# A kernel of gated linear attention and two expert layers: the prologue in another order, the first masks on ScalarE and GpSimd, products of ones ahead

## The chip, the cores and the metric

The kernel runs on one core of one Trainium2 chip. The metric is the device time of one execution in microseconds (us), the median of the runs shown. The engines are named as in the profile: PE is TensorE's matmuls, PEld its weight loads, DVE is VectorE, ACT ScalarE, POOL GpSimd, SP SyncE. SP issues nearly all transfers.

## What is computed

Three layers follow one another, on 3072 tokens (4 batches of 768) with 8 heads of 48:

```python
# 1. gated linear attention, per batch and head
f = sigmoid(f_logit)
for t in range(768):
    state = f[t][:, None] * state + outer(k[t], v[t])
    y[t] = q[t] @ state
# 2. dense layer, d_ff = 2048
h = maximum(x @ w_in, 0); x = (h * h) @ w_out
# 3. one of 8 experts per token (argmax of x @ w_gate), d_ff = 1024
out[mask] = gate[mask] * (maximum(x[mask] @ w1[e], 0) @ w2[e])
```

## The kernel before

**Tiling.** The tokens are cut into 24 chunks of 128 (`C`), and three chunks make a group of 384 (`G`); there are 8 groups. A chunk of attention is done in steps: `load_chunk` (f, q and k, v by SP), `sigmoid` (ScalarE, L210), `decays` (VectorE: two scans over 517 columns and a reciprocal, L216 to L225), `scale_qk` (VectorE, three products, keys first, L235 to L237), `scores` (TensorE: the keys' transposes into `pk`, L257, copied by ScalarE to `kt`, L259; then 16 products into two banks `pa`, L264), `masked` (VectorE multiplies both banks with a triangular mask into `at`, L271), `outputs` (TensorE: the queries with the state, L300, keys with values into `pu`, L310, values with masked scores into `py`, L320; then ScalarE's copies into `xT`, L328 to L333) and `state` (VectorE, L345 to L348). In group 0 the rows of heads 6 and 7 are brought to their places in `xT` by three products with the constant `spread` (L331); in later groups two small transfers xT<-xT do that (L336).

**The dense layer.** For each group `moe_h` makes 16 hidden blocks `ph` (L395 in group 0, where the weights are used whole; L405 in later groups, where weights and inputs are split into a high and a low part), `moe_act` squares their positive part on ScalarE (L411, L412), and `moe_out` adds them to `po` (L435), two blocks later. `ps_h` has two banks for hidden blocks, `ps_o` one for each of the three `po`, `ps_a` three that attention's steps share.

**Weights.** The dense weights come as 64 bit numbers in 16 jobs of 768 KB, alternately of `w_in` and `w_out`. `stage_job` loads one into one of three buffers `stg`, `convert_job` turns it into 32 bit with three VectorE instructions (L167, L170, L173) and has the next but two loaded into the buffer that it frees; `split_job` later splits it. Job 0 serves hidden blocks 0 and 1, job 1 their output blocks, job 2 hidden blocks 2 and 3, and so on.

**Order.** On TensorE, ScalarE, VectorE and GpSimd the order of this part is that of the program (`manual_schedule`, from L566 on); the constants ahead of it, and SP's queue in all of it, are ordered by the framework's planner. An engine works through its queue in order, so an instruction that waits holds all behind it. In the prologue chunks 0, 1 and 2 are done one after the other, with the first three conversions between the steps of chunk 2 and the decays, state and scaling that prepare chunk 3. Then group 0 of the dense layer runs, and the three chunks of the next group are threaded into its 16 blocks: `attention_group` waits for pairs (block, place in the block), and chunk 3 has its scores at block 1, chunks 4 and 5 at blocks 6 and 10; decays, outputs and scaling follow one, two and three blocks later. Each of blocks 0 to 12 of group 0 also converts one job (3 to 15). After job 15 the space of `stg` is freed and a table `wgb` of 1.5 MB is loaded (L787). At block 14 `split_x` splits the next group's `xT` into `xh` (ScalarE, L162) and `xl` (VectorE, L163).

## Time and profile before

| | us |
|---|---|
| median of three runs | 805.46 |
| the runs | 803.75, 805.46, 805.48 |
| the profiled execution | 804.5 |
| its span, first to last instruction | 802.8 |

The profile shows one execution. Its times are counted from the first instruction, so 1.7 us of the execution lie outside the span. A row of the timeline or of the chain begins with its start and its duration in us; what stands in brackets at its end is the idle time of the engine before it and what ended that.

### The profile page before, as it was taken

To read this page: it belongs to the slowest core of one execution; us is meant where nothing else is said; L and a number is where in the kernel's file an instruction comes from. 1 tells how busy PE (TensorE), PEld (TensorE's weight loads), DVE (VectorE), ACT (ScalarE), POOL (GpSimd) and SP (SyncE) were. 2 spreads that over 40 slices of the span, in tenths; PEclk is the share of its full clock that TensorE was granted. 3 is DMA by queue.
4 is the path that set the end of the run, shared out by engine and by line. 5 is a ranking of instruction groups with operands and counts; after the bars stand their busy time and mean duration, and the time that the engine had idled before them with its cause. 6 is when DMAs were issued, how large, how long until landed. Compare 5 with 4: busy or idle time off the path is not lost.

```text
span 802.8 us, 15135 instructions
## 1 busy us (share of the span) xinstructions
PE 775.1 (97%) x5657; PEld 723.2 (90%) x5657; DVE 561.3 (70%) x1309; ACT 413.4 (51%) x822; POOL 76.2 (9%) x108
## 2 busy tenths in 40 slices
PE   5899999999999999999999999999999999999994
PEld 4566579999999999999999999998999999999994
DVE  7999689768757767857757844668566676666650
ACT  2224376454464454455455454762566666666651
POOL 2000000000000000000000002000432232223110
PEclk9999999999999999999999999999999999999997
DMA  9787511111130121130120015321877777776760
GB/s 274 216 262 231 142 40 41 52 53 51 40 91 26 45 82 46 45 101 27 46 71 1 1 39 199 110 76 52 289 221 224 220 219 228 211 213 208 212 205 18
DMA packets 39410, 98.93 MB, mean 123 GB/s; under 512 B 5502, under 2 KB 9314, under 8 KB 39200
## 3 DMA queue, kind: packets, MB, share of 16 engines
q1 hardware_dynamic: 35744, 88.42, 37.3%
q0 software_dynamic: 3584, 9.46, 3.3%
q8 instruction: 46, 0.75, 0.4%
q14 instruction: 36, 0.29, 0.1%
HBM read 88.16 MB, written 10.24 MB: 123 GB/s over the span
## 4 chain that ended last, share of the span: by engine, by line
PE 85%; issue 6%; DVE 4%; DMA 2%; POOL 1%; ACT 1%; POOLq 0%; SPq 0%; DVEq 0%; ACTq 0%
PE po L435 25%; PE ph L405 23%; PE ph L982 11%; PE qo L1002 11%; PE ph L395 3%; PE pa L264 3%; PE py L320 3%; PE py L300 1%; PE pu L310 1%; DMA xT<-xT 1%; PE px L642 1%; PE pk L257 1%; DMA out<-o,ids 1%; PE pl L485 0%; DVE tl L216 0%
## 5 line engine op out<-in xcount | busy, mean ns | idle before, releaser
L411 ACT ACTIVATE gg<-ph 128x384 f32<-128x384 f32 x128 | 62.8, 491 | 184.6 <-PE ph L405 134.0
L614 DVE TENSOR_TENSOR w_lo<-raw,w_hi 128x768 fp32r<-128x768 f32 x112 | 107.0, 957 | 31.7 <-ACT w_hi L613 31.7
L418 DVE TENSOR_TENSOR gl<-gg,gh 128x384 fp32r<-128x384 f32 x112 | 62.1, 555 | 85.3 <-ACT gh L416 84.0
L405 PE MATMUL ph<-xh,w_lo 128*128 128x384 f32 x336 | 118.7, 353 | 0.9 <-ACT gg L411 0.9
L405 PE MATMUL ph<-xl,w_hi 128*128 128x384 f32 x336 | 114.4, 341 | 0.6 <-DVE xl L163 0.6
L405 PE MATMUL ph<-xh,w_hi 128*128 128x384 f32 x336 | 113.9, 339 | 0.0
L435 PE MATMUL po<-w_hi,gl 128*128 128x384 f32 x336 | 113.4, 338 | 0.0
L435 PE MATMUL po<-w_hi,gh 128*128 128x384 f32 x336 | 113.2, 337 | 0.0
L435 PE MATMUL po<-w_lo,gh 128*128 128x384 f32 x336 | 112.8, 336 | 0.0
L986 ACT ACTIVATE hh<-ph 128x256 fp32r<-128x256 f32 (+1 forms) x120 | 44.3, 370 | 103.3 <-PE ph L982 91.5
L613 ACT ACTIVATE w_hi<-raw 128x768 fp32r<-128x768 f32 x112 | 93.6, 837 | 0.0
L982 PE MATMUL ph<-xh,w_lo 128*128 128x256 f32 x312 | 88.9, 285 | 0.0
L982 PE MATMUL ph<-xl,w_hi 128*128 128x256 f32 x312 | 87.6, 281 | 0.0
L982 PE MATMUL ph<-xh,w_hi 128*128 128x256 f32 x312 | 87.5, 280 | 0.0
L459 DVE SCALAR_TENSOR_TENSOR junk<-rows,wgb 128x384 f32<-128x384 f32 x144 | 79.9, 555 | 3.3
L987 DVE SCALAR_TENSOR_TENSOR hl<-ph,hh 128x256 fp32r<-128x256 f32 (+1 forms) x120 | 48.7, 405 | 42.4 <-ACT hh L986 39.5
L1002 PE MATMUL qo<-w_hi,hl 128*128 128x384 f32 x208 | 70.4, 339 | 0.0
L1002 PE MATMUL qo<-w_hi,hh 128*128 128x384 f32 x208 | 70.4, 338 | 0.0
L1002 PE MATMUL qo<-w_lo,hh 128*128 128x384 f32 x208 | 70.1, 337 | 0.0
L412 ACT ACTIVATE gg<-gg 128x384 f32<-128x384 f32 x128 | 67.3, 526 | 4.1
L405 PEld LDWEIGHTS ph<-xh,w_lo 128*128 128x128 f32 x336 | 63.0, 188 | 6.9 <-issue 3.1
L405 PEld LDWEIGHTS ph<-xl,w_hi 128*128 128x128 f32 x336 | 63.1, 188 | 1.0 <-DVE xl L163 0.8
(235 smaller groups left out, 1498.0 us busy)
## 6 DMA issues: line engine op xcount, KB each, us to landing
raw<-w_e SPq DMA_DIRECT2D x120, 384.0 KB, 3.6
qk<-qk SPq DMA_DIRECT2D x46, 192.0 KB, 3.6
v<-vt SPq DMA_DIRECT2D x24, 256.0 KB, 3.7
stg<-w_in SPq DMA_DIRECT2D x8, 768.0 KB, 6.1
stg<-w_out SPq DMA_DIRECT2D x8, 768.0 KB, 6.0
f<-ft SPq DMA_DIRECT2D x24, 226.2 KB, 3.1
xs<-rows SPq DMA_DIRECT2D x8, 577.5 KB, 3.3
wgb<-w_gateT SPq DMA_DIRECT2D x1, 1536.0 KB, 7.1
```

Source lines behind the costliest of these rows:

```text
L405: nc.tensor.matmul(ph, lhsT=w[:, sl], rhs=x[:, k, :], start=(n == 0), stop=(n == 8))
L411: nc.scalar.activation(out=gg, in_=ph, func=AF.Relu)
L412: nc.scalar.activation(out=gg, in_=gg, func=AF.Square)
L418: nc.vector.tensor_tensor(out=gl, in0=gg, in1=gh.bitcast(F32), op=ALU.subtract)
L435: nc.tensor.matmul(po[m], lhsT=a[:, sl], rhs=w[:, ws], start=(i == 0 and n == 0), stop=(i == NF - 1 and n == len(terms) - 1),)
L459: nc.vector.scalar_tensor_tensor(out=junk, in0=rows[:, m, 0:DM], scalar=1.0, in1=wgb[0][:, e, :], op0=ALU.mult, op1=ALU.mult, accum_out=lg ...
L613: nc.scalar.activation(out=hi, in_=src, func=AF.Copy)
L614: eng.tensor_tensor(out=lo, in0=src, in1=hi.bitcast(F32), op=ALU.subtract)
L982: nc.tensor.matmul(ph, lhsT=wslice(s, w, (i * 3 + k) * 128, 128), rhs=x[:, k, :], start=(n == 0), stop=(n == 8))
L986: nc.scalar.activation(out=hh, in_=ph, func=AF.Relu)
L987: nc.vector.scalar_tensor_tensor(out=hl, in0=ph, scalar=0.0, in1=hh.bitcast(F32), op0=ALU.max, op1=ALU.subtract)
L1002: nc.tensor.matmul(out_t[s][m], lhsT=x[:, sl], rhs=wslice(s, w, 3 * F2 + i * DM, DM), start=(i == 0 and n == 0), stop=(i == 7 and n == 2),)
```

## The change

It does these things:

- Among the constants `step_r` and `step_f`, which the scans of `decays` read, come first on GpSimd, and `spread` after the masks.
- The input f of chunk 1 is loaded before v of chunk 0.
- `scores` is cut into `key_rows` (transposes and their copy) and `scores` (the 16 products), and `outputs` into `key_values`, `state_queries` and `scores_values`; the steps of the three first chunks then stand in a finer order, in which a chunk's products with `spread` come after the next chunk's scores.
- The outputs of the three first chunks go to the banks of `ps_o`, and their keys with values to the banks of `ps_h`, in place of `ps_a`. Row copies become three copies of 128 columns each.
- `masked` of chunks 0, 1, 3, 4 and 5 is done by two ScalarE copies and two GpSimd selects, in place of two VectorE products.
- 72 products of the constant `ones_bf` with itself stand first on TensorE, and 24 more before the values of chunk 0; nothing reads their results.
- The first three conversions stand together after chunk 2; decays 3 moves to block 0 of group 0, state 2 and the scaling of chunk 3 to block 1, and chunk 3's scores from block 1 to block 2.

The diff, without the loops that only moved into functions of their own:

```diff
--- before.py
+++ after.py
@@ -64,14 +64,13 @@
     xs = dram.tile([NT, ROW], F32, name="xs")
 
 
+    step_r = const.tile([PR, FL], BF16, name="step_r")
+    nc.gpsimd.memset(step_r, PFLOOR)
+    nc.gpsimd.memset(step_r[:, ::SEG], 1.0)
+    step_f = const.tile([PR, FL], F32, name="step_f")
+    nc.gpsimd.memset(step_f, PFLOOR)
     ident = const.tile([128, 128], F32, name="ident")
     make_identity(nc, ident)
-
-    spread = const.tile([128, 3, 128], F32, name="spread")
-    nc.gpsimd.memset(spread, 0.0)
-    for r in range(3):
-        for o in (0, 64):
-            nc.gpsimd.tensor_copy(spread[:, r, o + D : o + 64], ident[:, o + r : o + D : 3])
     mask = const.tile([128, 128], BF16, name="mask")
     nc.gpsimd.memset(mask, 1.0)
     nc.gpsimd.affine_select(
@@ -84,11 +83,12 @@
     )
     ones_bf = const.tile([128, 128], BF16, name="ones_bf")
     nc.vector.memset(ones_bf, 1.0)
-    step_r = const.tile([PR, FL], BF16, name="step_r")
-    nc.gpsimd.memset(step_r, PFLOOR)
-    nc.gpsimd.memset(step_r[:, ::SEG], 1.0)
-    step_f = const.tile([PR, FL], F32, name="step_f")
-    nc.gpsimd.memset(step_f, PFLOOR)
+
+    spread = const.tile([128, 3, 128], F32, name="spread")
+    nc.gpsimd.memset(spread, 0.0)
+    for r in range(3):
+        for o in (0, 64):
+            nc.gpsimd.tensor_copy(spread[:, r, o + D : o + 64], ident[:, o + r : o + D : 3])
     rev = const.tile([128, GC, NE], F32, name="rev")
     nc.gpsimd.iota(rev, pattern=[[0, GC], [-1, NE]], base=NE, channel_multiplier=0, allow_small_or_imprecise_dtypes=True)
     tok1 = const.tile([128, NCH], F32, name="tok1")
@@ -147,14 +147,22 @@
 
     ld_t = {}
 
+    def load_f(c):
+        f = ld.tile([PR, FL], F32, tag="f", name="f")
+        nc.sync.dma_start(out=f, in_=ft[c])
+        return f
+
+    f_t = {}
+
     def load_chunk(c):
         t = qk_t[c % 3]
-        f = ld.tile([PR, FL], F32, tag="f", name="f")
+        f = f_t.pop(c) if c in f_t else load_f(c)
         v3 = ld.tile([128, H, 64], F32, tag="v", name="v")
-        nc.sync.dma_start(out=f, in_=ft[c])
         for i in ((1, 2), (0, 1)) if c == 0 else ((0, 2),):
             for j in range(2):
                 nc.sync.dma_start(out=t[64 * j : 64 * j + D, slice(*i)], in_=qk[c, D * j : D * j + D, slice(*i)])
+        if c == 0:
+            f_t[1] = load_f(1)
         nc.sync.dma_start(out=v3, in_=vt[c])
         ld_t[c] = t, f, v3
 
@@ -247,9 +255,8 @@
 
     at_t = {}
 
-    def scores(c):
-        t, _, _ = ld_t[c]
-        qd, kd = t[:, 0], t[:, 1]
+    def key_rows(c):
+        kd = ld_t[c][0][:, 1]
         kt = None
         if c % CPB != CPB - 1:
             pk = ps_a.tile([128, 4, PR], F32, tag="att", name="pk")
@@ -257,84 +264,134 @@
                 nc.tensor.transpose(out=pk[:, p, :], in_=kd[:, p, :], identity=ident[0:PR, 0:PR])
             kt = a1.tile([128, 4, PR], F32, tag="kt", name="kt")
             nc.scalar.activation(out=kt, in_=pk, func=AF.Copy)
+        at_t[c] = kt, None
+
+    def scores(c):
+        t, _, _ = ld_t[c]
+        qd, kd = t[:, 0], t[:, 1]
         pas = [ps_a.tile([128, 4, 128], F32, tag="att", name="pa") for _ in range(2)]
         for p in range(4):
             for j in range(2):
                 rows = slice(64 * j, 64 * j + D)
                 nc.tensor.matmul(pas[j][:, p, :], lhsT=kd[rows, p, :], rhs=qd[rows, p, :], start=True, stop=True)
-        at_t[c] = kt, pas
+        at_t[c] = at_t[c][0], pas
+
 
     def masked(c):
         kt, pas = at_t[c]
         at = a1.tile([128, 2, 4, 128], F32, tag="at", name="at")
         for j in range(2):
-            nc.vector.tensor_tensor(
-                out=at[:, j], in0=pas[j], in1=mask[:, None, :].to_broadcast([128, 4, 128]), op=ALU.mult
-            )
+            if c in (0, 1, 3, 4, 5):
+                nc.scalar.activation(out=at[:, j], in_=pas[j], func=AF.Copy)
+                nc.gpsimd.affine_select(
+                    out=at[:, j],
+                    in_=at[:, j],
+                    pattern=[[0, 4], [1, 128]],
+                    compare_op=ALU.is_ge,
+                    fill=0.0,
+                    base=0,
+                    channel_multiplier=-1,
+                )
+            else:
+                nc.vector.tensor_tensor(
+                    out=at[:, j], in0=pas[j], in1=mask[:, None, :].to_broadcast([128, 4, 128]), op=ALU.mult
+                )
         at_t[c] = kt, at
 
 
...
+    def key_values(c, pu):
...
+    def state_queries(c, y, opens):
...
+    def scores_values(c, y, order, opens, closes):
+        _, _, v3 = ld_t.pop(c)
+        _, at = at_t.pop(c)
+        for n in order:
...
+    def outputs(c):
...
+        if not first:
+            state_queries(c, y, (0, 2))
+        if pu is not None:
+            key_values(c, pu)
+        scores_values(c, y, (2, 3, 0, 1), (0, 2) if first else (), (1, 3))
         ts = slice(m * C, (m + 1) * C)
         nc.scalar.activation(out=xT3[:, ts], in_=y[3], func=AF.Copy)
-        if g == 0:
-            for r in range(3):
-                nc.tensor.matmul(y[r], lhsT=spread[:, r, :], rhs=xT3[:, ts], start=False, stop=r > 0)
         nc.scalar.activation(out=xT[:, 2, ts], in_=y[2], func=AF.Copy)
         nc.scalar.activation(out=xT[:, 0:2, ts], in_=py[0], func=AF.Copy)
-        if m == GC - 1 and g:
+        if m == GC - 1:
             for o in (0, 64):
                 nc.sync.dma_start(out=xT[o + D : o + 64], in_=xT3[o : o + D])
+
+
+    first_y, first_pu = {}, {}
+
+    def first_banks(c):
+        po = [ps_o.tile([128, DM], F32, tag=f"po{m}", name="y") for m in range(GC)]
+        first_y[c] = [po[0][:, 0:C], po[0][:, C : 2 * C], po[2][:, 0:C], po[1][:, 0:C]]
+
+    def first_key_values(c):
+        first_pu[c] = pu = ps_h.tile([128, G], F32, tag="ph", name="pu")[:, 0 : 4 * D].rearrange(
+            "p (a b) -> p a b", a=4
+        )
+        key_values(c, pu)
+
+    def first_values(c, n=0):
+        y, ts = first_y[c], slice(c * C, (c + 1) * C)
+        for _ in range(n):
+            nc.tensor.matmul(y[3], lhsT=ones_bf, rhs=ones_bf, start=True, stop=True)
+        scores_values(c, y, (3, 2, 0, 1), () if c else (0, 2, 3), (3,))
+        nc.scalar.activation(out=x_t[0][1][:, ts], in_=y[3], func=AF.Copy)
+
+    def first_rows(c):
+        xT, xT3 = x_t[0]
+        y, ts = first_y[c], slice(c * C, (c + 1) * C)
+        for r in range(3):
+            nc.tensor.matmul(y[r], lhsT=spread[:, r, :], rhs=xT3[:, ts], start=False, stop=r > 0)
+        for r in (2, 0, 1):
+            nc.scalar.activation(out=xT[:, r, ts], in_=y[r], func=AF.Copy)
 
     def state(c, pu):
         if pu is None:
@@ -361,13 +418,22 @@
     def attention_group(g):
         for m in range(GC):
             c = g * GC + m
-            b = (1, 6, 10)[m] if g == 1 else 5 * m
+            b = (2, 6, 10)[m] if g == 1 else 5 * m
+            if c == GC:
+                while not (yield) == (0, 1):
+                    pass
+                decays(c)
+                while not (yield) == (1, 1):
+                    pass
+                state(c - 1, first_pu.pop(c - 1))
+                scale_qk(c)
             while not (yield) == (b, 1):
                 pass
             if m == 0:
                 x_tiles(g)
             if 4 < c + 2 < NCH:
                 load_chunk(c + 2)
+            key_rows(c)
             scores(c)
             masked(c)
             sigmoid(c + 1)
@@ -571,36 +637,51 @@
     stage_job(1)
     stage_job(2)
     nc.sync.dma_start(out=wg, in_=w_gate)
+
+    idle = ps_h.tile([128, G], F32, tag="ph", name="idle")
+    for _ in range(72):
+        nc.tensor.matmul(idle[:, 0:128], lhsT=ones_bf, rhs=ones_bf, start=True, stop=True)
     x_tiles(0)
     sigmoid(0)
     sigmoid(1)
     decays(0)
     scale_qk(0)
+    key_rows(0)
     scores(0)
-    sigmoid(2)
     decays(1)
     masked(0)
-    pu = outputs(0)
+    first_key_values(0)
+    sigmoid(2)
     scale_qk(1)
-    state(0, pu)
+    state(0, first_pu[0])
+    key_rows(1)
+    first_banks(0)
+    first_values(0, 24)
     scores(1)
     decays(2)
     masked(1)
-    pu = outputs(1)
+    first_rows(0)
+    first_key_values(1)
     scale_qk(2)
-    state(1, pu)
+    state(1, first_pu[1])
+    first_banks(1)
+    state_queries(1, first_y[1], (0, 2, 3))
+    first_values(1)
+    key_rows(2)
     scores(2)
+    masked(2)
+    first_rows(1)
+    first_key_values(2)
+    first_banks(2)
+    state_queries(2, first_y[2], (0, 2, 3))
+    first_values(2)
+    first_rows(2)
     load_chunk(3)
     convert_job(0)
-    masked(2)
-    pu = outputs(2)
-    sigmoid(3)
     load_chunk(4)
     convert_job(1)
-    decays(3)
-    state(2, pu)
-    scale_qk(3)
     convert_job(2)
+    sigmoid(3)
     job = 3
 
     ph2 = ExitStack()
```

## Rows read from the trace of the kernel before

**Rows 1.** The page, part 4: shares of the chain that ended last, by engine.

```profile
PE 85%; issue 6%; DVE 4%; DMA 2%; POOL 1%; ACT 1%; POOLq 0%; SPq 0%; DVEq 0%; ACTq 0%
```

**Rows 2.** Timeline to 13 us: start, duration, engine, line, operation, tiles, forms, releaser.

```profile
4.10 0.64 ACT L210 ACTIVATE f<-f 112x517 f32<-112x517 f32 x1 [2.00 <-DMA f<-ft]
...
5.70 0.11 POOL L89 MEMSET step_r<- 112x5 bf16 x1
...
5.85 1.24 DVE L216 TENSOR_TENSOR_SCAN tl<-f,step_r 112x517 f32<-112x517 f32 x1 [1.46 <-POOL step_r L89]
...
9.93 1.23 DVE L216 TENSOR_TENSOR_SCAN tl<-f,step_r 112x517 f32<-112x517 f32 x1
...
12.57 1.26 DVE L271 TENSOR_TENSOR at<-pa,mask 128x512 f32<-128x512 f32 x2
```

**Rows 3.** The chain in order of time, 30 to 42 us: start, duration, what.

```profile
30.58 1.25 DVE tl L216
...
33.86 0.69 DVE qk L235
...
37.82 2.17 PE ph L395 x6
...
41.93 1.93 PE ph L395 x6
```

**Rows 4.** The same chain: TensorE's blocks of the chunks, and one of group 1.

```profile
18.18 1.90 PE pa L264 x16
...
28.55 0.66 PE py L331 x4
...
45.80 0.60 PE py L300 x16
...
46.40 0.54 PE pu L310 x13
...
46.94 0.95 PE py L320 x16
...
59.69 0.39 PE pk L257 x4
...
60.08 1.09 PE pa L264 x16
...
108.56 1.60 PE ph L405 x8
```

**Rows 5.** Timeline from 79 to 104 us, the end of group 0.

```profile
79.05 1.16 PE L264 MATMUL pa<-qk 48*128 48x128 f32 x16
...
81.45 1.23 DVE L216 TENSOR_TENSOR_SCAN tl<-f,step_r 112x517 f32<-112x517 f32 x1
...
89.95 0.35 SPq L787 DMA_DIRECT2D wgb<-w_gateT  x1
...
99.48 2.10 PE L435 MATMUL po<-w_raw,gg 128*128 128x384 f32 x6
...
100.86 1.16 ACT L162 ACTIVATE xh<-xT 128x1152 fp32r<-128x1152 f32 x1 [7.14 <-DMA xT<-xT]
...
102.06 1.36 DVE L163 TENSOR_TENSOR xl<-xT,xh 128x1152 fp32r<-128x1152 f32 x1 [7.35 <-ACT xh L162]
```

**Rows 6.** Groups of GpSimd instructions by form: count, busy us, mean ns of one.

```profile
masks.py:199 POOL TENSOR_SCALAR_AFFINE_SELECT ident<-ident 128x128 f32<-128x128 f32 x1 | 0.3, 282 | 0.0
```

**Rows 7.** Timeline, 37 to 41 us: first instructions of two successive conversions.

```profile
37.59 0.55 DVE L167 TENSOR_SCALAR w_raw<-stg 128x768 uint32<-128x768 uint32 x1
...
40.05 0.55 DVE L167 TENSOR_SCALAR w_raw<-stg 128x768 uint32<-128x768 uint32 x1
```

**Rows 8.** Instructions of tile `stg` up to 110 us: time from issue to landing.

```profile
DMA to landing us min/median/max: 4.4/6.1/9.9
```

**Rows 9.** Windows at the end: length, busy (count) by engine, PEclk, DMA, GB/s.

```profile
791.00:792.00 1.00, 0.47 (x3) 0.14 (x1) 0.00 (x0) 0.50 (x1) 0.00 (x0) 1.00 0.11 25
...
794.00:795.00 1.00, 0.00 (x0) 0.00 (x0) 0.00 (x0) 0.00 (x0) 0.00 (x0) 0.78 0.30 94
```

More of the change, by code (lines that the diff above doesn't have):

```diff
@@ L270, in masked @@
         for j in range(2):
-            nc.vector.tensor_tensor(
-                out=at[:, j], in0=pas[j], in1=mask[:, None, :].to_broadcast([128, 4, 128]), op=ALU.mult
-            )
-        at_t[c] = kt, at
+            if c in (0, 1, 3, 4, 5):
[13 more added lines that the diff above has]
+                )
+        at_t[c] = kt, at
+    def key_values(c, pu):
+        kt, _ = at_t[c]
+        v3 = ld_t[c][2]
+        for p in range(4):
+            for j in range(2):
+                nc.tensor.matmul(
+                    pu[64 * j : min(64 * j + 64, PR), p, :],
+                    lhsT=kt[:, p, 64 * j : min(64 * j + 64, PR)],
+                    rhs=v3[:, p + 4 * j, 0:D],
+                    start=True,
+                    stop=True,
+                )
+    def state_queries(c, y, opens):
+        qd = ld_t[c][0][:, 0]
+        for s in range(2):
+            for b in range(2):
+                for j in range(2):
+                    rows, p = slice(64 * j, 64 * j + D), 2 * s + b
+                    nc.tensor.matmul(
+                        y[2 * j + s][64 * b : 64 * b + 64],
+                        lhsT=wst[c % 2][rows, p, :],
+                        rhs=qd[rows, p, :],
+                        start=2 * j + s in opens,
+                        stop=False,
+                    )
+    def scores_values(c, y, order, opens, closes):
+        _, _, v3 = ld_t.pop(c)
+        _, at = at_t.pop(c)
+        for n in order:
+            for b in range(2):
+                j, p = n // 2, 2 * (n % 2) + b
+                nc.tensor.matmul(
+                    y[n][64 * b : 64 * b + 64],
+                    lhsT=v3[:, p + 4 * j, :],
+                    rhs=at[:, j, p, :],
+                    start=n in opens,
+                    stop=n in closes,
+                )
     def outputs(c):
@@ L279, in outputs @@
         first = c % CPB == 0
-        t, _, v3 = ld_t.pop(c)
-        qd = t[:, 0]
-        kt, at = at_t.pop(c)
         xT, xT3 = x_t[g]
@@ L290, in outputs @@
         y = [py[0][:, 0, :], py[0][:, 1, :], py[1][:, 0, :], py[1][:, 1, :]]
-        if g == 0:
-            y[2] = ps_o.tile([128, DM], F32, tag=f"po{m}", name="y2")[:, 0:C]
-        opens = (0, 2, 3) if g == 0 else (0, 2)
-        closes = (3,) if g == 0 else (1, 3)
         if not first:
-            for s in range(2):
-                for b in range(2):
-                    for j in range(2):
-                        rows, p = slice(64 * j, 64 * j + D), 2 * s + b
-                        nc.tensor.matmul(
-                            y[2 * j + s][64 * b : 64 * b + 64],
-                            lhsT=wst[c % 2][rows, p, :],
-                            rhs=qd[rows, p, :],
-                            start=2 * j + s in opens,
-                            stop=False,
-                        )
-        if pu is not None:
-            for p in range(4):
-                for j in range(2):
-                    nc.tensor.matmul(
-                        pu[64 * j : min(64 * j + 64, PR), p, :],
-                        lhsT=kt[:, p, 64 * j : min(64 * j + 64, PR)],
-                        rhs=v3[:, p + 4 * j, 0:D],
-                        start=True,
-                        stop=True,
-                    )
-        for n in (2, 3, 0, 1):
-            for b in range(2):
-                j, p = n // 2, 2 * (n % 2) + b
-                nc.tensor.matmul(
-                    y[n][64 * b : 64 * b + 64],
-                    lhsT=v3[:, p + 4 * j, :],
-                    rhs=at[:, j, p, :],
-                    start=first and n in opens,
-                    stop=n in closes,
-                )
+            state_queries(c, y, (0, 2))
+        if pu is not None:
+            key_values(c, pu)
+        scores_values(c, y, (2, 3, 0, 1), (0, 2) if first else (), (1, 3))
         ts = slice(m * C, (m + 1) * C)
         nc.scalar.activation(out=xT3[:, ts], in_=y[3], func=AF.Copy)
-        if g == 0:
-            for r in range(3):
-                nc.tensor.matmul(y[r], lhsT=spread[:, r, :], rhs=xT3[:, ts], start=False, stop=r > 0)
         nc.scalar.activation(out=xT[:, 2, ts], in_=y[2], func=AF.Copy)
         nc.scalar.activation(out=xT[:, 0:2, ts], in_=py[0], func=AF.Copy)
-        if m == GC - 1 and g:
+        if m == GC - 1:
             for o in (0, 64):
@@ L337, in outputs @@
         return pu
+    first_y, first_pu = {}, {}
[5 more added lines that the diff above has]
+            "p (a b) -> p a b", a=4
+        )
+        key_values(c, pu)
[12 more added lines that the diff above has]
+            nc.scalar.activation(out=xT[:, r, ts], in_=y[r], func=AF.Copy)
     def state(c, pu):
```

## The prediction

> **What bounds the kernel now.** I read the chain of waits first, by engine: 85% of the span hangs on TensorE [rows 1], so a change to the first 35 of 803 us can give back no more than the time in which TensorE waits there, and only what is not lost again later. So I then read the chain in order of time and the timeline through the first 105 us, and asked at each step which wait ends last. Three stretches come out.
>
> (a) Up to 37.8 us the chain runs mostly over VectorE: the decays of chunk 0 cannot start before a constant is written by GpSimd [rows 2]; then decays, scalings, masks and weight conversions follow one another, and the dense layer stops until the third conversion has ended, so that its third hidden block (`ph`) starts at 37.82 and its fourth at 41.93 [rows 3]. TensorE's own blocks in that stretch are short, but at two speeds: the same 16 score products (`pa`) take 1.90 us at 18.18 and 1.09 us at 60.08 [rows 4]. That ratio, 1.74, is the clock's low level against its high one, with what does not scale.
>
> (b) From 41.93 to about 92 us the chain is TensorE alone, one block behind the other; VectorE is nearly full but a step ahead.
>
> (c) At the end of group 0 the chain leaves TensorE. The last conversion frees the staging space, at 89.95 the 1.5 MB table `wgb` is issued, and the small copy xT<-xT, which group 1 needs, lands behind it at 100.8; ScalarE waits for that 7.14 us, VectorE's split ends at 102.06+1.36 = 103.42, and only then do group 1's products run, though the dense layer's last block ended near 99.48+2.10 = 101.58 [rows 5]. So 1.8 us are lost to a transfer, and a gain made earlier meets this wait before it reaches the end.
>
> **The change part by part.** I follow one quantity, the start of the fourth hidden block (41.93 before): at that point both orders have done three hidden blocks, one output block, and key rows and scores of chunk 3.
>
> *Constants first.* Sigmoid 0 ends at 4.10+0.64 = 4.74, but the decays start at 5.85, held by the second write of `step_r` [rows 2]. With `step_r` first on GpSimd they start at 4.80: 1.05 us gained. What moves behind (ident, mask, spread, the iotas) is not wanted before 8 us. On SP's queue f(1) moves ahead of v(0): VectorE came to decays 1 at 9.93 without waiting [rows 2] and now comes 1.05 us sooner; the move covers that, and without cover it would cost 1.05 at most. v(0) is one issue later and wanted near 10 us: nothing.
>
> *VectorE to the keys of chunk 1.* Decays and scaling: 9.93-5.85 = 4.08; decays alone: 12.57-9.93 = 2.64 [rows 2]. So decays 1 at 8.88, and, the mask of chunk 0 being gone, the scaling of chunk 1 at 11.52, its keys (0.69, the row at 33.86 [rows 3]) ready at 12.2. The mask now takes two ScalarE copies, which I price at 0.6 (the 517 column sigmoid takes 0.64 [rows 2]), and two GpSimd selects of 512 columns. One of 128 takes 0.28 [rows 6]; bounds 0.28 and 4 x 0.28 = 1.13. Overhead is about the 0.11 of the five column write at 5.70 [rows 2], so I take 0.11+4 x 0.17 = 0.8. For chunk 0 all that ends near 12.5, before TensorE wants it at 14.2.
>
> *TensorE in the prologue.* Beside this work, 72 products of ones run before the first keys (at 8.2). Their rows do not exist. A product of 384 columns takes 1.60/8 = 0.20 in the split layers [rows 4], so 0.067 for 128 columns at the high level and twice that at the low one: 72 take 4.8 to 9.6 us from 1.1, ending at 5.9 to 10.7. Chunk 0's products have about 2 us to spare, so I take nothing. If they do what they look like, chunk 1's blocks run at the high level. From 12.2: key rows 0.39, 24 more ones 24 x 0.067 = 1.6, values 0.95, scores 1.09, spread rows 6/4 x 0.66 = 1.0, key values 0.54, a wait of some 0.3 (an estimate: three short copies queue behind the two mask copies), state queries 0.60, values 0.95, key rows 0.39, scores 1.09 [rows 4]: 8.9 us, so the scores of chunk 2 end at 21.1. The select for chunk 1 ends near 18.5 and is wanted at 18.7: just in time.
>
> *VectorE from there.* Its own work on chunks 1 and 2 is done at 11.52+1.44+0.3+2.64+1.44 = 17.3 (scaling, a short state, decays, scaling), and but for 0.64 of state 1 it then waits for key values and scores, 3.3 us in all: this is where the gain of the prologue goes. From 21.2: mask of chunk 2 1.26 [rows 2], five conversions of 40.05-37.59 = 2.46 [rows 7] (12.3, since conversions 3 and 4 now stand ahead of the state of chunk 2), decays 3 and state 2 33.86-30.58 = 3.28, keys 0.69 [rows 3]: 17.5 us, to 38.7. Conversion 3 would start 4.9 us after its load is issued; such loads took 4.4 to 9.9, median 6.1 [rows 8]. The wait is 0 to 1.2 at the median; as nothing else is due there I take 0.3. Keys of chunk 3 ready: 39.0.
>
> *TensorE meanwhile.* Scores 2 end at 21.1; rows, key values, queries, values, rows and the last copies put the first hidden block at 26.3. Only one bank of `ps_h` is free until state 2, so hidden blocks 1 and 2 each wait about 0.7 for ScalarE; all three and one output block are done by 35.9, and TensorE then stands 3.2 us before chunk 3's keys. That hides the 1.4 of the banks, and would have to be paid if the keys came early. Fourth hidden block: 39.0+0.1+0.39+1.09+0.1 = 40.7, against 41.93: **1.2 us gained**.
>
> *Group 0.* From here TensorE has the same blocks in both, so everything moves by 1.2. Masks 3 to 5 leave VectorE (3.8 us less); it is not what ends last there, so that gives nothing. But for chunk 5 it costs: sigmoid 6 stands behind two mask copies on ScalarE, and decays 6 behind sigmoid 6. Scores 5 ended at 79.05+1.16 = 80.21 and decays 6 began at 81.45 [rows 5]; now scores end at 79.0, copies and sigmoid add 0.6+0.6+0.64, decays 6 begin at 80.85. From decays 6 to the issue of `wgb` it is 8.5 us as before, so the issue, the landing of xT and the start of group 1 move by **0.6 us**; TensorE's end (100.4) is not late. After that nothing differs.
>
> Sum: 804.5 (the profiled run; its span is 802.8) less 0.6 is 803.9. The three timed runs have a median of 805.46, 1.0 above the profiled one; from there, **804.9**.
>
> **Where a page speaks against the change.** The rows: TensorE's last products lie in the us from 791 (0.47 of it busy, granted clock 1.00); from 794 to 795 the mean is 0.78 [rows 9], so in that us the clock fell from its 2.4 to its 1.2 GHz level, after some 3 us of idling. The Trainium skill, "TensorE: Matmul & The Clock Gate", section "Why this matters for your kernels", warns of such idle gaps between bursts, and puts the price at the half rate. By that rule the 3.2 us gap would undo the gain; without it, the sum above stands.
>
> GpSimd's rows here run beside VectorE's plain writes only. The Trainium skill, "GPSIMD Engine Reference", section "Specifications", says its SBUF interface is shared with VectorE instructions that have two SBUF inputs, and decays and scalings are such. By it the selects would be longer than 0.8, which is rival 4; no row of this case shows the two side by side.
>
> **The rivals.**
> 1. *The clock falls in the new gap.* For: the gap of 3.2 us is as long as the idling after which the clock fell at the end [rows 9]. Against: it is no longer, and an error of half a us ends it. Price: the low pace lasted before from the first keys, somewhat ahead of 9.93 [rows 2], to at least 20.08 [rows 4], 10 us with pauses; half of that, 5.0, is the upper bound, 0 the lower; dense blocks have no pauses, so I take 2.5: 807.4. Above a loss of 3.0 it is slower by the bound below.
> 2. *The ones do not hold the high level* (the side opposite to the forecast). Between the ones and chunk 1's keys TensorE works about 2.5 us and idles 1.5. If the clock stays low until about 20 us, as before [rows 4], key rows, ones, values, scores of chunk 1 (4.0 us) cost 74% more, 3.0, and rows and key values (1.54) 1.1: VectorE waits that much longer for the scores of chunk 2, and all behind it moves: 804.9+4.1 = 809.0. It decides from 3.0 of delay on.
> 3. *xT overtakes.* SP's order is not by hand. If it changes so that xT is issued ahead of `wgb`, group 1 starts at TensorE's end: 103.42-100.4 = 3.0 gained on 805.46, 802.5. For: conversion 15 now comes 0.6 us later against chunk 5's values. Against: at 89.95 `wgb` was first although it was ready last [rows 5].
> 4. *The selects are slow.* At 1.7 each, twice my price, the mask of chunk 1 ends at 16.8+3.4 = 20.2, 1.5 late, and moves all behind it: 806.4. Against: no row has them so long.
> 5. *The change doesn't do what it says:* the second `step_r` write is again put late, 3.75 us behind the first; 1.05 is lost: 806.0.
>
> **How the numbers follow.** Below 0.3%, 2.4 us, no difference can be told. Chances: forecast 0.50, rival 1 0.20, rival 2 0.08, rival 3 0.10, rival 4 0.05, rival 5 0.07. Faster by over 0.3%, under 803.0: 0.07 of rival 3 and 0.04 of the forecast (if conversion 3 doesn't wait and spans are shorter). Slower, above 807.9: rival 2, 0.09 of rival 1, 0.03 from rival 4 and the forecast. Together 0.11 and 0.20. The rest, 0.69, is the same. Range: from 802.6 to 808.2; below lies half of rival 3, above it rival 2 and a quarter of rival 1, some 0.18.
>
> **What would show it.** Right: decays 0 at 4.8; 16 score products of chunk 1 in about 1.1; VectorE idle about 3.3 before the mask of chunk 2, which starts at 21.2; first hidden block near 26; TensorE idle some 3 us before chunk 3's key rows at 39; fourth hidden block at 40.7; `wgb` still ahead of xT, group 1 near 102.8. Wrong: score products of 1.9, dense blocks of about 4 us behind the gap, xT landing near 93, or a prologue in which conversions stand closer than 17.5 us.

## The result, and the profile after

| | before | after |
|---|---|---|
| median, us | 804.61 | 811.17 |
| the runs, us | 803.28 to 805.48 | 810.33 to 812.75 |
| the profiled execution, us | 804.5 | 810.33 |
| its span, us | 802.8 | 808.5 |

The median before is now that of four runs, where the three known ahead gave 805.46. The ratio is 1.0078, 95% interval 1.0056 to 1.0100: slower by 6.3 us (6.6 between the medians), where 0.6 us of gain was forecast. The time lies above the range.

The loss is there by the fourth hidden block and its output block, and nearly all of it stays: the spans differ by 5.7 us. TensorE's timeline from 33 to 53 us (a row: start, duration, engine, line, operation, tiles, forms; in brackets the idle time before it and what ended that):

```profile
33.60 2.20 PE L461 MATMUL ph<-xT,w_raw 128*128 128x384 f32 x6 [0.58 <-ACT gg L477]
35.64 2.10 PE L501 MATMUL po<-w_raw,gg 128*128 128x384 f32 x6
42.61 1.01 PE L264 MATMUL pk<-ident,qk 112*128 112x112 f32 x4 [4.87 <-DVE qk L243]
43.54 2.08 PE L276 MATMUL pa<-qk 48*128 48x128 f32 x16
45.55 4.21 PE L461 MATMUL ph<-xT,w_raw 128*128 128x384 f32 x6
49.55 2.40 PE L501 MATMUL po<-w_raw,gg 128*128 128x384 f32 x6
51.79 2.10 PE L461 MATMUL ph<-xT,w_raw 128*128 128x384 f32 x6
```

TensorE stands still for 4.87 us before the key rows of chunk 3, and its next three blocks run at about half pace: by the chain, which counts a block from the end of the one before, key rows take 1.01 and scores 2.01 against 0.39 and 1.09 [rows 4], the fourth hidden block 4.14 against 1.93 [rows 3]. The windows there (length, then busy time of PE, PEld, DVE, ACT and POOL with the number of instructions, granted clock, DMA share, GB/s):

```profile
39.00:40.00 1.00, 0.00 (x0) 0.00 (x0) 0.96 (x2) 0.00 (x0) 0.00 (x0) 0.95 1.01 387
40.00:41.00 1.00, 0.00 (x0) 0.00 (x0) 0.96 (x2) 0.00 (x0) 0.00 (x0) 0.50 0.19 72
...
49.00:50.00 1.00, 1.00 (x3) 0.59 (x2) 1.00 (x1) 0.20 (x1) 0.00 (x0) 0.50 0.64 246
50.00:51.00 1.00, 1.00 (x4) 0.56 (x3) 0.97 (x3) 0.81 (x2) 0.00 (x0) 0.93 0.02 6
```

The granted clock is 1.00 while TensorE ends its output block at 37.74 and idles into the 40th us; then it is 0.50, the 1.2 GHz level, up to 50 us, with TensorE at work again since 42.61. What held the keys back is in the chain of waits (start, duration, what):

```profile
27.23 6.42 DMA stg<-w_out
...
33.68 0.57 DVE w_raw L175
...
36.22 1.16 DVE tl L224
...
38.85 0.46 DVE w_raw L175
...
39.34 0.97 DVE w_raw L178
...
41.87 0.69 DVE qk L243
...
42.61 1.01 PE pk L264 x4
```

VectorE's queue has conversion 3 (`w_raw`, from 33.68) and conversion 4 (from 38.85) ahead of the keys, and conversion 3 waits 1.56 us for its load, as VectorE's timeline has it:

```profile
33.68 0.56 DVE L175 TENSOR_SCALAR w_raw<-stg 128x768 uint32<-128x768 uint32 x1 [1.56 <-DMA stg<-w_out]
```

In the chain the loss adds up so. The late keys cost 2.16 us: at the high clock the fourth hidden block would have begun at 42.61+0.39+1.09 = 44.09, against 41.93 before. The slow key rows and scores cost 1.53 (the block began at 45.62), and the slow fourth hidden block and its output block 2.46 (4.14+2.19 in the chain against 1.93+1.94): 6.15 us in all. Group 1's second product starts 5.83 us later, 109.30 against 103.47, in both as soon as the split has ended (102.06+1.36 in [rows 5]):

```profile
96.70 0.35 SPq L868 DMA_DIRECT2D wgb<-w_gateT  x1
...
106.69 1.16 ACT L170 ACTIVATE xh<-xT 128x1152 fp32r<-128x1152 f32 x1 [6.81 <-DMA xT<-xT]
...
107.88 1.36 DVE L171 TENSOR_TENSOR xl<-xT,xh 128x1152 fp32r<-128x1152 f32 x1 [7.02 <-ACT xh L170]
...
109.30 0.44 PE L471 MATMUL ph<-xl,w_hi 128*128 128x384 f32 x1 [0.57 <-DVE xl L171]
```

The prologue did part of what it should. Rows of three engines from its timeline:

```profile
4.77 1.26 DVE L224 TENSOR_TENSOR_SCAN tl<-f,step_r 112x517 f32<-112x517 f32 x1 [0.36 <-ACT f L218]
...
5.13 3.06 POOL L91 COPY spread<-ident 128x16 f32<-128x16 f32 x6
...
7.47 0.66 DVE L243 TENSOR_TENSOR qk<-qk,tl 112x512 f32<-112x512 f32 x1
...
8.23 0.57 PE L264 MATMUL pk<-ident,qk 112*128 112x112 f32 x4 [0.70 <-POOL spread L91]
...
10.65 2.45 POOL L286 TENSOR_SCALAR_AFFINE_SELECT at<-at 128x512 f32<-128x512 f32 x2 [2.46 <-ACT at L285]
...
11.55 1.05 DVE L243 TENSOR_TENSOR qk<-qk,tl 112x512 f32<-112x512 f32 x1
...
12.53 1.11 DVE L244 TENSOR_TENSOR qk<-qk,f 112x512 f32<-112x512 f32 x1
...
12.71 0.98 PE L264 MATMUL pk<-ident,qk 112*128 112x112 f32 x4 [2.16 <-issue]
...
13.48 2.72 PE L384 MATMUL y<-ones_bf 128*128 128x128 bf16 x24
...
19.07 1.22 POOL L286 TENSOR_SCALAR_AFFINE_SELECT at<-at 128x512 f32<-128x512 f32 x2 [5.96 <-ACT at L285]
...
23.47 1.29 DVE L296 TENSOR_TENSOR at<-pa,mask 128x512 f32<-128x512 f32 x2 [2.89 <-PE pa L276]
```

The decays start at 4.77, 1.08 us earlier. But beside a VectorE that now works, GpSimd's six copies into `spread` take 3.06 us. The profile puts TensorE's idle 0.70 us before the first key rows down to them, as they ended last, at 8.19; but the keys of chunk 0 were scaled only at 7.47+0.66 = 8.13, so the copies cost 0.1 us at most. In before, with VectorE waiting, the same six took 0.90:

```profile
4.86 0.90 POOL L74 COPY spread<-ident 128x16 f32<-128x16 f32 x6
```

Two selects beside VectorE's last scan and scaling take 2.45 us, and the scaling 1.05 and 1.11; the next two selects, with no such neighbour, take 1.22. And 12.6 to 16 us is a second stretch of low clock, with key rows of 0.98 and the 24 ones in 2.51 by the chain (the window from 10 to 15 us grants 0.76). So mask 2 stands at 23.47.

### The profile page after: what moved, and what is told of

Same layout as the page of the kernel before. It is cut to its first block, busy times and chain, and to the rows that moved or that the text cites. A ratio compares the mean times of both kernels' runs of the same rounds, so it can differ in the third digit from the quotient of the medians.

```text
span 808.5 us, 15344 instructions
## 1 busy us (share of the span) xinstructions
PE 783.5 (97%) x5753; PEld 729.6 (90%) x5753; DVE 555.9 (69%) x1299; ACT 418.9 (52%) x835; POOL 86.2 (11%) x118
## 4 chain that ended last, share of the span: by engine, by line
PE 87%; issue 4%; DVE 3%; DMA 2%; POOL 1%; ACT 1%; POOLq 0%; SPq 0%; DVEq 0%; ACTq 0%
PE po L501 24%; PE ph L471 23%; PE ph L1063 12%; PE qo L1083 12%; PE pa L276 3%; PE ph L461 3%; PE py L337 2%; PE py L323 1%; PE pu L307 1%; PE pk L264 1%; PE px L723 1%; DMA xT<-xT 1%; DMA stg<-w_out 1%; PE pl L551 0%; POOL out L1096 0%
```

## The experiments

The theory after the result: *the keys of chunk 3 stand behind conversions 3 and 4 in VectorE's queue; TensorE runs dry, and the clock that falls there takes as much again*. The rivals: the clock is no cost of its own; the masks on other engines or the ones make the loss. Each ratio below is against runs of before on the same chip, whose medians were 805.0 to 805.7 us.

**Two fillings of the gap.** TensorE is kept busy ahead of chunk 3's key rows.

```diff
+            if c == GC:
+                fill = ps_a.tile([128, 4, 128], F32, tag="att", name="fill")
+                for _ in range(80):        # 150 in the second
+                    nc.tensor.matmul(fill[:, 0, :], lhsT=ones_bf, rhs=ones_bf, start=True, stop=True)
             key_rows(c)
             scores(c)
```

> The changed kernel with 80 more products of ones on TensorE just ahead of chunk 3's key rows, in the 4.9 us in which it idled; their results are read by nothing. Theory A (the idling ahead of chunk 3's keys lets the clock fall, and the low level costs key rows and scores 1.5 us and the fourth hidden block 2.2): the score products of chunk 3 take about 1.1 us in place of 2.0, the fourth hidden block 1.9 to 2.1 in place of 4.1, the time is 3.7 lower, about 807.5. Rival B (the late keys alone make the loss, the clock's share is hidden by the later wait for xT): 811, no change. Either way 2 to 3 us over before should stay, since the keys are as late as in the changed kernel.

812.44 us, ratio 1.0089 [1.0062, 1.0115]: not told apart from after. In the profiled execution the load of conversion 3 landed 2.6 us later than in after, so the key rows began at 45.21, the 80 products were over 2.97 us before, and the clock fell in that rest.

> After, with 150 products of ones (128 x 128, read by nothing) on TensorE ahead of the key rows of chunk 3. 150 of them cover about 8.6 us at the high clock, longer than the gap of 4.87 us plus the later load that the shorter filling met. Theory A (the low clock behind the gap costs 1.5 us in key rows and scores and 2.2 us in the fourth hidden block): granted clock stays at 0.99 or more from 38 to 50 us, key rows of chunk 3 about 0.39 us, its scores about 1.1, the fourth hidden block about 1.9 to 2.2; time falls by up to 3.7 us to 807.5 to 808.5, less whatever the filling delays the keys past the point where VectorE has them. Rival B (the clock is not what costs; it is the late keys alone): the clock is high there and the time stays at 810 to 812.

810.22 us, ratio 1.0055 [1.0037, 1.0072]: 0.9 us under after by the medians and 1.9 by the ratios, with intervals that overlap, where up to 3.7 was expected. Its timeline:

```profile
37.42 8.54 PE L439 MATMUL fill<-ones_bf 128*128 128x128 bf16 x150
45.79 0.55 PE L264 MATMUL pk<-ident,qk 112*128 112x112 f32 x4
46.28 1.16 PE L276 MATMUL pa<-qk 48*128 48x128 f32 x16
47.37 2.20 PE L465 MATMUL ph<-xT,w_raw 128*128 128x384 f32 x6
```

The blocks behind the filling run at the high clock (granted 1.00 from 20 to 55 us). The keys were again late: conversion 3 began at 36.62 behind a wait of 4.65, 2.9 us later than in after, and the filling outlasted even these keys by 0.4. From the start of chunk 3's key rows to the end of the fourth hidden block it is 3.62 us in the chain here (45.95 to 49.57) and 7.15 in after (42.61 to 49.76): the low clock cost 3.5 us there. Rival B falls for that stretch, by its rows. The total alone would not refute it (it expected 810 to 812): it moved less because the keys moved the other way.

**The keys back in their old place** (decays 3, state 2 and the scaling ahead of conversion 2, chunk 3's scores at block 1; all else as in after):

```diff
     convert_job(1)
-    convert_job(2)
     sigmoid(3)
+    decays(3)
+    state(2, first_pu[2])
+    scale_qk(3)
+    convert_job(2)
```

> The changed kernel with one part undone: decays 3, state 2 and the scaling of chunk 3 stand again ahead of conversion 2 in the prologue, and chunk 3's scores again at block 1. Theory A (what costs is the order on VectorE, five conversions ahead of chunk 3's keys, and the idling that follows): keys of chunk 3 at about 33.6, no idling of 3 us on TensorE, no low clock after it, fourth hidden block at 40.5 to 41.5, time 803.5 to 805. Rival C (the prologue's own parts cost, that is GpSimd's selects beside VectorE, or the products of ones): the third conversion ends as late as before or later and the time stays over 807.

803.96 us, ratio 0.9988 [0.9975, 1.0000]. The loss is gone with this one move. What is left over:

```profile
35.24 3.63 PE L453 MATMUL ph<-xT,w_raw 128*128 128x384 f32 x6 [1.37 <-DVE w_raw L181]
```

Now the third hidden block waits for conversion 2, as it did in before [rows 3], and here it also meets a low clock (0.68 granted from 35 to 40 us).

**The move alone, in before:** decays 3 in block 0, state 2 and the scaling in block 1, scores at block 2.

```diff
-            b = (1, 6, 10)[m] if g == 1 else 5 * m
+            b = (2, 6, 10)[m] if g == 1 else 5 * m
+            if c == GC:   # wait for (0, 1), decays(c), wait for (1, 1), state(c - 1, pu), scale_qk(c)
...
-    decays(3)
-    state(2, pu)
-    scale_qk(3)
     convert_job(2)
```

> Before, with the one move alone: decays 3 in the first hidden block, state 2 and the scaling for chunk 3 in the second, and the scores of chunk 3 behind the third. Theory: the keys of chunk 3 come behind conversions 3 and 4, TensorE idles 4 to 6 us ahead of them, the granted clock falls, key rows 1.0, scores 2.0, fourth hidden block 3.7 to 4.2 us, and the time is 4 to 7 us above before (809 to 812), about what the whole change costs. Rival (the mutual slowing of GpSimd and VectorE and the later second mask in the prologue make the loss): this run is within 1.5 us of before.

809.93 us, ratio 1.0056 [1.0038, 1.0074]: most of the change's 1.0078, from one part of it. The rows are those of after again, but that the key rows still ran at the high clock:

```profile
41.83 0.57 PE L257 MATMUL pk<-ident,qk 112*128 112x112 f32 x4 [4.28 <-issue]
42.48 2.08 PE L264 MATMUL pa<-qk 48*128 48x128 f32 x16
44.48 4.21 PE L403 MATMUL ph<-xT,w_raw 128*128 128x384 f32 x6
```

**The masks.** All of them on VectorE (`if c in ():` in `masked`), else as after:

> The changed kernel with all masks on VectorE again. Theory A: VectorE loses 1.25 us to each of two masks in the prologue but the two scalings of chunk 1 go back from 2.2 to 1.35 us, and the second mask falls into a wait: keys of chunk 3 within 1 us of the changed kernel's 42.6, time within 1.5 of 811. Rival C (ScalarE and GpSimd make the masks late): the scores of chunk 2 end 2 us sooner, time 808 or less.

813.27 us, ratio 1.0105 [1.0069, 1.0141]: not better than after, so ScalarE's and GpSimd's masks are not the loss. VectorE's scaling of chunk 1 is at 0.68 here, with no select beside it, which shows whose work slowed it.

**The third place for the keys:** behind conversion 2, ahead of conversions 3 and 4; the scores of chunk 3 stay at block 2.

```diff
     convert_job(1)
     convert_job(2)
     sigmoid(3)
+    decays(3)
+    state(2, first_pu[2])
+    scale_qk(3)
     job = 3
```

(and the waits for (0, 1) and (1, 1) with these three steps go from `attention_group`).

> After, with decays 3, state 2 and the scaling for chunk 3 taken out of the first chunk's generator and put right behind conversion 2, ahead of conversions 3 and 4; the scores of chunk 3 stay behind the third hidden block. Theory (the keys behind conversions 3 and 4 are the whole loss, and VectorE reaches them 2.46 + 1.56 + 2.46 us earlier): keys scaled near 36 us, TensorE idle less than 1 us ahead of them, scores of chunk 3 about 1.1 us, fourth hidden block ends by 42.5 us, the time 802 to 803.5, 0.3 % under before. Rival: the hidden blocks 3 and 4 then wait for conversions 3 and 4 and the load of stage 3, and the time is 804 to 806, no better than before.

801.76 us, ratio 0.9957 [0.9943, 0.9972]: faster than before by 0.43%. VectorE's and TensorE's rows:

```profile
33.73 0.68 DVE L243 TENSOR_TENSOR qk<-qk,tl 112x512 f32<-112x512 f32 x1
...
35.34 0.56 DVE L175 TENSOR_SCALAR w_raw<-stg 128x768 uint32<-128x768 uint32 x1 [0.24 <-DMA stg<-w_out]
...
35.99 0.55 PE L264 MATMUL pk<-ident,qk 112*128 112x112 f32 x4
36.47 1.16 PE L276 MATMUL pa<-qk 48*128 48x128 f32 x16
37.56 2.20 PE L453 MATMUL ph<-xT,w_raw 128*128 128x384 f32 x6
```

The load of conversion 3 is no earlier than in after, but what VectorE does meanwhile is the work on the keys, so the wait is 0.24; TensorE finds the keys ready, and the fourth hidden block starts 8 us earlier than in after, 4.3 earlier than in before. This execution had no stretch of low clock in the prologue; one of the same order that had it (the run with named banks, below) starts that block at 39.01.

> The same order as in the run before this one in the list, with the masks of chunks 3 to 5 back on VectorE (those of chunks 0 and 1 stay on ScalarE and GpSimd). If GpSimd's selects in chunks 3 to 5 are hidden: equal to it within 0.2 %. If they sit on the path of scores to values: faster by the difference of a select chain and a VectorE mask, some 0.5 us a chunk, 801 to 802. If VectorE is the late engine there: slower by up to 1.26 us a chunk, 805 to 807.

802.68 us, ratio 0.9963 [0.9948, 0.9977]. Its one further edit is `if c in (0, 1):` in `masked`. Within the intervals the masks of chunks 3 to 5 may stand on either engine.

**Is it the order or the prologue?** Before, with conversion 2 ahead of those three steps and chunk 3's scores at block 2:

```diff
-            b = (1, 6, 10)[m] if g == 1 else 5 * m
+            b = (2, 6, 10)[m] if g == 1 else 5 * m
...
+    convert_job(2)
     decays(3)
     state(2, pu)
     scale_qk(3)
-    convert_job(2)
```

> Before, with one thing altered: conversion 2 stands ahead of decays 3, state 2 and the scaling for chunk 3, and the scores of chunk 3 come behind the third hidden block. Theory A (most of the gain of that order is that the third hidden block no longer waits for conversion 2, which in before released it at 37.8): first three hidden blocks 29.5 to 35.6, keys of chunk 3 near 35, fourth hidden block near 39.1 instead of 41.8, time 2 to 3 us under before, 802.5 to 803.5 if before is at 805.6. Rival B (the gain needs the finer prologue): within 1 us of before.

801.66 us, ratio 0.9967 [0.9950, 0.9984]. That much of order, in before, is not told apart from the same with the whole new prologue around it: a gain of the other parts of the change is not shown. The chain:

```profile
29.33 6.07 PE ph L395 x18
35.40 1.94 PE po L435 x6
37.34 0.39 PE pk L257 x4
37.72 1.09 PE pa L264 x16
38.81 2.13 PE ph L395 x6
```

Three hidden blocks run without a pause, and the fourth starts 3.1 us before the 41.93 of [rows 3]; 0.7 of that was there at the first one (29.33 against 30.07).

**All masks on VectorE in the better order** (`if c in ():`):

> The order with decays 3, state 2 and the scaling for chunk 3 behind conversion 2, and all masks on VectorE. Theory A (the masks of chunks 0 and 1 on ScalarE and GpSimd shorten the way from the scores to the values, and GpSimd's selects slow VectorE by 0.8 us in chunk 1's scaling): VectorE's masks of 1.26 us for chunks 0 and 1 come back into its queue, less 0.8, so mask 2 comes 1 to 2 us later and the time is 802.5 to 804. Rival B (those engines were no help, since VectorE waited 2.8 us ahead of mask 2 anyway): 801.5 to 802.2.

804.06 us, ratio 0.9976 [0.9963, 0.9990], over the kernel with ScalarE's and GpSimd's masks by 2.3 us of the medians and 1.5 of the ratios, with intervals that just overlap. With the keys in their better place the masks may be worth something: mask 2 stands at 25.14 here, 21.89 there. Part of that is the clock, granted at 0.57 from 15 to 20 us here and 1.00 there; in the run with named banks, where it fell too, mask 2 stands at 23.34.

**34 more ones**, in the idle time before chunk 1's key rows:

```diff
+    first_banks(0)
+    for _ in range(34):
+        nc.tensor.matmul(first_y[0][3], lhsT=ones_bf, rhs=ones_bf, start=True, stop=True)
     key_rows(1)
-    first_banks(0)
```

> The order with decays 3, state 2 and the scaling for chunk 3 behind conversion 2, and 34 further products of ones (read by nothing) on TensorE between the state update of chunk 0 and the key rows of chunk 1, where TensorE idled 2 us (10.7 to 12.7) in four profiles and the clock stood low from 12.6 to 16 us in three of the four. Theory A (that idle time is what the clock falls on): 34 products end near 12.7, the granted clock is at 0.97 or more from 10 to 30 us, mask 2 at 21.9, the time 800.4 to 801.4 with a spread under 2 us. Rival B (the level in 12.6 to 16 does not hang on that gap, or it does not reach the end): 801.8, as without them.

800.87 us (799.92 to 801.48), ratio 0.9948 [0.9930, 0.9965]: the lowest of all, and below both kernels; from the 801.76 without them it is not told apart. Chunk 1's key rows took 0.58 and the 24 ones 1.34, the pace of the high clock. That the 34 ones hold it is not shown: the profile without them had 0.57 and 1.34.

**What the ones are worth.** Four kernels have fewer of them. In after, without the 72 and the 24 and their tile, then with one product left:

> The changed kernel without the 72 and the 24 products of ones. Theory A: the clock is low until some 18 to 20 us; chunk 1's blocks take about 1.8 us longer, but 2.5 us of ones are gone from their chain; scores of chunk 2 within 1 us of 23.4, time 810 to 812. Rival D (the ones are what makes the prologue fast): scores of chunk 2 3 us later and the time near 814.

> After, with a single product of ones where 72 were and none of the 24, the tile kept. Theory A (the late keys and the low clock behind the gap make the loss, and the clock in the prologue reaches the end only by the 0.3 to 1 us that mask 2 comes later): keys of chunk 3 near 43, TensorE idle 3 to 5 us ahead of them, fourth hidden block about 4 us, the time 811 to 812.5. Rival B (the ones themselves bring on the low clock behind the gap): granted clock at 0.9 or more from 40 to 50 us and the time under 809.

811.35 us, ratio 1.0076 [1.0052, 1.0100], and 809.90, ratio 1.0059 [1.0043, 1.0076]: like after. But TensorE stands in another place. In both the third hidden block waits, 6.95 and 6.98 us, for VectorE's state 2 (L404), which like the keys is behind conversions 3 and 4; the key rows then follow without a pause. The second of the two:

```profile
41.02 4.21 PE L461 MATMUL ph<-xT,w_raw 128*128 128x384 f32 x6 [6.98 <-DVE wst L404]
```

So these totals do not price the ones. Chunk 0's and chunk 1's scores run at about 2 us in both (1.16 in after), so the ones do bring the high clock earlier in the prologue; but the keys come no later for it, and the ones do not bring on the low clock behind the gap: at 40 to 45 us it is 0.50 in the second of these too. The same two edits in the better order:

> The same order without any products of ones (72 and 24 left out). Theory A (the ones hold the clock high at the start, and with no gap left behind the third hidden block this reaches the end): the clock is low to about 20 us, mask 2 near 23.8, and the time is 1 to 2.5 us over that with the ones, 803 to 804.5. Rival B (their price and their gain cancel, as without them in the order of the change): within 0.8 us of it, 801 to 802.6.

> The order with decays 3, state 2 and the scaling for chunk 3 behind conversion 2, with a single product of ones where 72 were and none of the 24: unlike the two kernels without any, the tile that the ones write is still there, so that the two banks of the hidden blocks take the same turns and the second hidden block does not wait for state 2's bank (4.84 us in one of those, 6.95 in the other). Theory A (the ones hold the clock): granted clock low to about 20 us, mask 2 near 22.9 against 21.9, first hidden block 27.4 against 26.5, the time 802.4 to 803.5 against 801.8 with the ones. Rival B (the ones are worth the 5.8 us that leaving them and their tile out cost): 806.5 to 808. Rival C (worth nothing): 801.3 to 802.2.

807.55 us, ratio 1.0028 [1.0011, 1.0045], and 807.64, ratio 1.0030 [1.0019, 1.0042]: 5.8 us over the kernel with all ones, which no term for the clock explains. The timeline of the one without any:

```profile
27.41 2.20 PE L453 MATMUL ph<-xT,w_raw 128*128 128x384 f32 x6 [0.54 <-ACT xT L394]
34.46 5.76 PE L453 MATMUL ph<-xT,w_raw 128*128 128x384 f32 x12 [4.84 <-DVE wst L404]
```

The second hidden block waits 4.84 us for VectorE's state 2 (L404): it was given the bank of chunk 2's key-value products, where in the kernel with all ones it followed the first hidden block in the same bank. My first reading, that the missing tile shifted the turns, fell with the run that kept it and waited 4.83. So the banks were named by hand:

```diff
-    ps_h = ... bufs=2        # every tile there had the tag "ph"
+    ps_h = ... bufs=1
-        first_pu[c]: tag="ph"
+        first_pu[c]: tag=f"ph{(1, 0, 1)[c]}"
-        ph: tag="ph"
+        ph: tag=f"ph{0 if n < 3 else n % 2}"     # n counts the hidden blocks
```

> The order with decays 3, state 2 and the scaling for chunk 3 behind conversion 2, all 72 and 24 products of ones, and the banks of the hidden blocks named by hand: chunk 2's key-value products in the second bank, the first three hidden blocks in the first, then in turns. That is how they fell in the kernel of that order whose second hidden block started at 29.24 us. The control for the next run: 801 to 802.5, as that kernel (801.76).

> The same with a single product of ones where 72 were and none of the 24. The second hidden block cannot take the bank of state 2 any more. Theory A (the ones are worth what the clock of the prologue gives, about 1 us at mask 2; the 5 us more that the kernels with fewer ones took came from the bank): second hidden block 0.6 us behind the first, no stretch of low clock behind 25 us, the time 0.6 to 2 us over the control, 802 to 804. Rival B (the ones themselves are worth the 5.8 us): 806 to 808.

801.80 us with all ones (800.03 to 802.46), ratio 0.9944 [0.9923, 0.9965]; 802.69 with one (801.23 to 804.54), ratio 0.9967 [0.9948, 0.9987]. The second hidden block of the latter:

```profile
30.15 2.20 PE L457 MATMUL ph<-xT,w_raw 128*128 128x384 f32 x6 [0.58 <-ACT gg L473]
```

So about 4.9 of those 5.8 us were the bank (807.64 less 802.69), with the low clock behind its wait in them (0.51 granted from 35 to 40 us in that kernel). The ones are worth 0.9 by the medians, 1.9 by the ratios, with intervals that overlap: no worth of theirs is shown. That the bank given depends on the number of ones is seen only through these waits; why it does, the traces do not tell.

## Why the prediction was wrong

- **Constants first: right.** Decays 0 at 4.77 (4.80 forecast). What moved behind was "not wanted before 8 us", as forecast, but narrowly: GpSimd and VectorE now work side by side, and `spread` was done at 8.19, 0.06 behind the keys of chunk 0.
- **Keys of chunk 1:** 12.6 instead of 12.2, because the selects slowed the scaling (1.05 for 0.67). The selects were priced at 0.8 each; they took 0.63 alone, and 1.42 and 1.08 beside VectorE. That is rival 4's mechanism, at less than its 1.7, and its own price was not paid: both masks were done before TensorE wanted them.
- **TensorE in the prologue: a term mis-sized.** 8.9 us forecast from chunk 1's key rows to the end of scores 2; it was 10.7 (12.71 to 23.42). Of the 1.8 us more, 0.6 lie in the key rows and 0.9 in the 24 ones, both at the low clock. Rival 2 happened for 3.5 us of the prologue, not to 20 us. With the late start that put mask 2 at 23.47 instead of 21.2; in the two profiles of the same prologue without that stretch of low clock it stood at 21.89. VectorE idled ahead of it for 1.96 and 2.89 us, 4.9 in all where 3.3 was forecast.
- **VectorE from there: a second term mis-sized.** 17.5+0.3 us forecast from mask 2 to the keys; it was 19.1. Of the 1.3 us more, 1.26 are the wait of conversion 3 for its load, put at 0.3 because "nothing else is due there"; but the DMA engines were busy for 0.90 of the time from 25 to 30 us and for all of it from 30 to 35. In the eight profiles in which that conversion waited for its load it began between 32.85 and 37.05. So the keys came at 42.6, not 39.0: 2.3 of these 3.6 us from the prologue, 1.3 from the load.
- **The gap: right in kind.** Hidden blocks 1 and 2 waited 0.58 each for the bank, the first came at 28.0 instead of 26.3, and TensorE stood 4.87 us, forecast 3.2.
- **The step that failed: the blocks behind the gap stood in the sum at the high clock** ("39.0+0.1+0.39+1.09+0.1 = 40.7", then "the same blocks in both"). They took 1.01, 2.01, 4.14 and 2.19 us for 0.39, 1.09, 1.93 and 1.94. Up to that output block a gain of 1.2 us was forecast and a loss of 6.15 measured; of the 7.4 between them the clock is 4.0, and the late keys are the rest. The late keys alone would have left the time inside the range (805.46+2.16 = 807.6).
- **Rival 1 is what happened**, at a chance of 0.20 and a price of 2.5. The gap came out 1.7 us longer than forecast, so "an error of half a us ends it" was the wrong side to look at: both errors above pushed the other way. Nor was a shorter gap shown to be safe: in the prologue of after the clock fell near 12.6 us, after 2.0 us of idling (from 10.55). The price was 4.0 by the rows (1.53+2.46, the output block in it) and 3.5 up to that block by the filled gap; the 2.5 was the middle of a bound worked from the prologue, not the blocks that stood behind the gap, the first three at about twice their time. The rule quoted beside it from the Trainium skill, "TensorE: Matmul & The Clock Gate", section "Why this matters for your kernels", is borne out for this gap: granted clock 0.50 behind it, 1.00 with it filled.
- **Group 0 and `wgb`: right.** The table went ahead of xT, whose wait was 6.81 for 7.14, and what was lost by 52 us reached group 1 with 0.3 taken off (5.83 of 6.15).
- **What was not asked:** whether the move was needed. Conversion 2 ahead of decays 3 is all that frees the third hidden block; with that and chunk 3's scores at block 2, in before alone, the kernel is 0.33% faster. The change moved the three steps two conversions too far.

## What to carry to other kernels

When steps change places in an in-order queue, list what each moved step now stands behind, and treat an instruction that waits for a load as long as its latest landing, not its median: work that another engine needs goes ahead of it. Where a sum leaves TensorE an idle stretch near one after which its clock was seen to fall, cost the blocks behind it at about twice their time in the main forecast. Before pricing an instruction by taking it out, look whether a later tile then waits for another buffer, since here that was 4.9 of 5.8 us.

## What the runs showed that I had not expected

- GpSimd and VectorE slow each other, in both directions. Copies of 128x16 took 0.55 us each in the mean beside scans and scaling and 0.19 beside an idle VectorE; VectorE's product with two SBUF inputs took 1.05 to 1.11 when it began beside a select of 128x512 and 0.68 without. A scan already under way kept its 1.24, and the select that began beside it took 1.42 in place of 0.63; a scan that began in the last 0.25 us of a select took 1.33, and 1.64 in the last 0.55 (the second filling). In these rows the instruction that began second paid. The Trainium skill, "GPSIMD Engine Reference", section "Specifications", names that sharing and those instructions; the trace agrees, for the products and for the scans.
- Products whose results nothing reads can change which bank a later tile gets: fewer products of ones, with the rest of the program alike, made a hidden block wait 4.8 to 7.0 us in four kernels.
- The same prologue ran with a stretch of low clock (12.6 to 16 us in after) in some profiles and without it in others: the granted clock from 10 to 15 us was 0.73 to 0.87 in five of that prologue and 1.00 in two, where the 24 ones took 1.34 us.
- The granted clock of a window is to be read with the pace of its products: from 5 to 20 us it is 1.00 in before and in the kernels with one product of ones, where chunk 0's and chunk 1's scores took 1.9 to 2.1 us (1.16 at the high clock).
